# Gate vectors as matmul columns spread by DMA, six shared score sets in the first chunk, an output tail in halves, and a new order

## The chip, the cores and the metric

One core of a Trainium2 chip. The metric is the device time of one execution in microseconds (us), lower is better. The kernel before takes 344.02 us (median of 3 runs, 342.9 to 345.37). TensorE does the matmuls, ScalarE the exponentials and tanh, VectorE and GpSimd the elementwise work. SyncE issues all transfers (DMA), in order, from one queue.

## The reference

```python
mod = (silu(c) @ w_mod).reshape(1, 6, 1, -1)          # c: 1 x 640, w_mod: 640 x 3840
sa, ca, ga, sb, cb, gb = six vectors of 640           # shift, scale, gate, twice
h = layernorm(x) * (1 + ca) + sa                      # x: 2048 x 640, bf16
x = x + ga * (window_attention(h) @ wo)               # 32 heads of 20, each row sees the last 256
h = layernorm(x) * (1 + cb) + sb
x = x + gb * ((sigmoid(h @ w_gate) * (h @ w_up)) @ w_down)   # 640 -> 1536 -> 640
```

The two gate vectors `ga` and `gb` multiply columns of the output, so the kernel multiplies them once into the weights `wo` and `w_down`. For that it keeps each gate copied to all 128 partitions of SBUF (`gbc`, 128 x 640).

## The kernel before

The kernel is a list of operations with what each reads and writes. A planner in the program places them, before anything runs, on the five engines with a model of their durations. Among those that are ready it takes the one with the lowest number in a table of priorities, `TIMES`. The result is a fixed order per engine. Each engine's program is in that order, with waits on semaphores of the others, so a late transfer stops an engine at the first instruction that needs it, and all that stands behind it.

A gate was made on all partitions at once: the left operand is silu(c) copied to 128 columns, so the result has 128 equal rows.

```python
def mod_bc(wm, c0, factor, prio):
    for half in range(2):
        ps = Tile(p_M, "modb")                               # one of three accumulator banks
        ... five matmuls: silubc[:, kt, :] (128x128) by wm[:, kt, 320 columns] -> ps (128x320)
        A("dve", tensor_scalar(gbc[:, 320 columns], ps, factor, mult))
```

The shift and scale vectors are made as columns (`mod_cols`): 25 matmuls of 64 columns, each with a 128 x 128 block of `w_mod` as weights, so that value number t*128 + p lands in partition p, column t. Then come the products with the weights, on whichever of two engines the planner finds free:

```python
for t in range(5):
    A(("pool", "dve"), tensor_tensor(wo[:, t, :], wo[:, t, :], gbc, mult), reads=[wo loads, gbc], tag="wos")
```

The scores of an attention chunk go through one score buffer (four banks) in sets. q and k go to DRAM as `dq<-stg`, `dk<-stg` and come back in another layout, from a few staging buffers `stg`. Attention output goes out as `doc<-On` and comes back as `oT<-doc`. Twenty warm-up matmuls (`S<-Tn`), from 1.36 to 9.3 us in the profile, keep TensorE busy while the first loads are on their way.

The softmax here doesn't subtract the row's maximum and nothing guards it: scores larger than these inputs give would overflow.

## Time and profile before

| | before |
|---|---|
| median time | 344.02 us (3 runs) |
| span of the profiled execution | 339.9 us, mean granted clock (share of TensorE's full speed) 0.999 |
| TensorE busy | 330.0 us, 97% |
| first projection matmul | 13.20 us |
| waits of TensorE | 3.8 us before 14 us, 2.8 us after |
| landing of 128 KB `dq<-stg`, 160 KB `x` | 3.2 us, 4.1 us |

A landing is the time from the issue of a transfer to its completion, as the median over its kind. Two lines of the page's part on DMA issues: the columns are what goes where, the issuing engine, how many, the size of each, and the median landing in us. In all lines of the profile PE is TensorE, DVE VectorE, ACT ScalarE, POOL GpSimd, and SPq the queue of SyncE; L and a number is a line of the kernel.

```profile
x<-in_A_x_dram SPq DMA_DIRECT2D x32, 160.0 KB, 4.1
...
dq<-stg SPq DMA_DIRECT2D x15, 128.0 KB, 3.2
```

The reader is to keep 3 to 5 us in mind as what such transfers take in this kernel: in the busy stretch from 60 to 90 us the medians are 5.0 us for `dq<-stg` and 3.4 for `x`.

### The profile page before, as it was taken

What the parts mean: (1) busy time and instruction counts of PE and PEld (TensorE: products, weight loads), DVE (VectorE), ACT (ScalarE), POOL (GpSimd) and SP (SyncE); (2) the same over time, 40 slices, a digit from 0 to 9 for tenths busy, and PEclk for the clock granted to TensorE, in tenths of its full rate; (3) what the DMA queues carried; (4) which work ended last, traced back from release to release, by engine and by line L of the source; (5) the groups of instructions that cost most, each with busy time, mean ns of one, the idle gap of its engine ahead of it and who ended that gap; (6) DMA issues with size and microseconds to landing.
All of it is one profiled execution on the core that took longest, in us unless ns stands there. A gap on an engine that the chain in (4) does not pass through costs nothing.

```text
span 339.9 us, 9584 instructions
## 1 busy us (share of the span) xinstructions
PE 330.0 (97%) x3813; PEld 201.2 (59%) x3813; DVE 227.6 (67%) x493; ACT 226.9 (67%) x229; POOL 178.4 (52%) x301
## 2 busy tenths in 40 slices
PE   7799989999999999998999999999999999999996
PEld 2577646655555656564765433466545446788884
DVE  4576599999776889646977446398746874554432
ACT  1377878888888888896887798956678851022230
POOL 5132564797666999555675566656656850010000
PEclk9999999999999999999999999999999999999999
DMA  6966689889987752472064101302740122112101
GB/s 211 353 202 181 191 235 257 288 270 209 231 282 253 224 194 41 151 226 60 2 180 115 48 31 65 111 3 40 162 123 12 49 22 72 44 35 41 39 3 39
DMA packets 50990, 44.99 MB, mean 132 GB/s; under 512 B 16513, under 2 KB 46850, under 8 KB 50946
## 3 DMA queue, kind: packets, MB, share of 16 engines
q1 hardware_dynamic: 50946, 44.38, 45.4%
q8 instruction: 30, 0.49, 0.6%
q14 instruction: 14, 0.11, 0.1%
HBM read 28.90 MB, written 12.19 MB: 121 GB/s over the span
## 4 chain that ended last, share of the span: by engine, by line
PE 92%; DMA 4%; SPq 1%; DVE 1%; ACT 1%; issue 0%; ACTq 0%; DVEq 0%
PE M L842 74%; PE S L843 8%; PE O L843 7%; PE M L843 3%; DMA big<-in_w_mod_dram 2%; DMA oT<-doc 1%; SPq L764 1%; DMA doc<-On 1%; ACT hT L984 0%; DVE x L937 0%; DVE V L1020 0%; DVE hT L1005 0%; ACT stg L1019 0%; DVE x L1316 0%; DVE big L1306 0%
## 5 line engine op out<-in xcount | busy, mean ns | idle before, releaser
L1188 ACT ACTIVATE E<-S 128x2048 bf16<-128x2048 f32 (+1 forms) x64 | 118.0, 1844 | 20.9 <-PE S L843 19.6
L842 PE MATMUL M<-h2T,wgu 128*128 128x256 bf16 (+1 forms) x720 | 114.6, 309 | 0.0
L842 PEld LDWEIGHTS M<-h2T,wgu 128*128 128x128 bf16 x720 | 67.2, 98 | 36.6 <-issue 5.5
L1199 POOL TENSOR_SCALAR_AFFINE_SELECT E<-E 128x512 bf16<-128x512 bf16 x89 | 59.9, 683 | 23.3 <-ACT E L1188 21.6
L1201 POOL TENSOR_SCALAR_AFFINE_SELECT E<-E 128x512 bf16<-128x512 bf16 x78 | 50.4, 655 | 31.8 <-ACT E L1188 27.5
L1306 DVE SCALAR_TENSOR_TENSOR big<-sig,M 128x256 bf16<-128x256 f32 (+1 forms) x72 | 36.4, 506 | 41.7 <-PE M L842 20.2
L1304 ACT ACTIVATE sig<-M 128x256 f32<-128x256 f32 (+1 forms) x72 | 32.4, 452 | 44.1 <-PE M L842 43.5
L842 PE MATMUL M<-wd,big 128*128 128x320 bf16 x384 | 56.5, 299 | 0.0
L842 PEld LDWEIGHTS M<-wd,big 128*128 128x128 bf16 x384 | 36.5, 98 | 16.0 <-issue 1.7
L843 PE MATMUL S<-QT,KT 20*128 20x256 bf16 (+2 forms) x832 | 36.2, 258 | 0.0
L926 DVE BATCH_NORM_STATS2 st<-x 128x6 f32<-128x320 bf16 x64 | 27.3, 477 | 7.2 <-DMA x<-in_A_x_dram 7.1
L1249 DVE STREAM_TRANSPOSE T<-O 128x512 f32<-128x512 f32 x32 | 22.6, 708 | 12.6 <-PE O L843 12.5
L843 PEld LDWEIGHTS S<-QT,KT 20*128 20x128 bf16 x832 | 12.3, 92 | 26.5 <-ACT E L1188 9.4
L1316 DVE TENSOR_TENSOR x<-M,x 128x320 bf16<-128x320 f32 x32 | 15.5, 484 | 18.3 <-PE M L842 17.8
L842 PE MATMUL M<-wv,hT 128*128 128x320 bf16 x160 | 27.4, 300 | 0.0
L842 PE MATMUL M<-wo,oT 128*128 128x320 bf16 x160 | 25.8, 300 | 1.5 <-DMA oT<-doc 1.4
L932 POOL TENSOR_SCALAR st<-st 128x2 f32<-128x2 f32 (+1 forms) x11 | 3.0, 274 | 40.4 <-DVE st L929 40.4
L842 PE MATMUL M<-hT,wk 128*128 128x512 bf16 (+1 forms) x100 | 23.1, 354 | 1.1 <-DVE V L1020 1.0
L1258 DVE STREAM_TRANSPOSE On<-Tn 128x512 bf16<-128x512 bf16 x32 | 22.5, 704 | 0.5
L842 PE MATMUL M<-hT,wq 128*128 128x512 bf16 (+1 forms) x100 | 22.7, 356 | 0.0
L843 PE MATMUL O<-E,V 128*32 128x256 bf16 (+2 forms) x568 | 21.1, 262 | 0.0
L1019 ACT ACTIVATE stg<-M 128x512 bf16<-128x512 f32 (+1 forms) x31 | 16.5, 534 | 6.6 <-PE M L842 6.2
(85 smaller groups left out, 386.3 us busy)
## 6 DMA issues: line engine op xcount, KB each, us to landing
x<-in_A_x_dram SPq DMA_DIRECT2D x32, 160.0 KB, 4.1
big<-in_w_mod_dram SPq DMA_DIRECT2D x15, 320.0 KB, 5.5
doc<-On SPq DMA_DIRECT2D x16, 256.0 KB, 2.2
KT<-dk SPq DMA_DIRECT2D x6, 512.0 KB, 5.1
QT<-dq SPq DMA_DIRECT2D x6, 512.0 KB, 4.7
out_dram<-x SPq DMA_DIRECT2D x16, 160.0 KB, 1.8
wgu<-in_B_w_gate_dram SPq DMA_DIRECT2D x5, 384.0 KB, 4.1
dq<-stg SPq DMA_DIRECT2D x15, 128.0 KB, 3.2
```

Of the source, the lines that this page charges most:

```text
L842: return e.matmul(o, l, r, start=st, stop=sp, skip_group_check=True)
L843: return e.matmul(o, l, r, start=st, stop=sp, tile_position=tp, skip_group_check=True)
L926: ins = e.bn_stats(v(bi * 12 + j * 6, 6), src[bi].ap[:, j * 320:(j + 1) * 320])
L1019: return e.activation(dst(), src(), ACT.Copy)
L1188: A("act", lambda e, eng, E=E, Sp=Sp, ncol=ncol: e.activation(E.ap[:, :, 0:ncol], Sp.ap[:, :, 0:ncol], ACT.Exp, scale=SM_SCALE), c_act(4 * ...
L1199: return e.affine_select(ap, ap, pattern=[[0, 4], [1, 128]], compare_op=ALU.is_ge, fill=0.0, base=0, channel_multiplier=-1)
L1201: return e.affine_select(ap, ap, pattern=[[0, 4], [-1, 128]], compare_op=ALU.is_ge, fill=0.0, base=-1, channel_multiplier=1)
L1249: A("dve", lambda e, g: e.transpose(T1.ap[:], O.ap[:]), 0.71, reads=[O.r()], writes=[T1.r()], prio=4, tag="tr1")
L1258: A("dve", lambda e, g: e.transpose(On.ap[:, half * 512:half * 512 + 512], Tn.ap[:]), 0.71, reads=[Tn.r()], writes=[On.r(half)], prio=7, t ...
L1304: A("act", lambda e, g, pg=pg, sg=sg: e.activation(sg.ap[:, 0:W], pg.ap[:, 0:W], ACT.Tanh, scale=0.5), c_act(W), reads=[pg.r()], writes=[s ...
L1306: A("dve", lambda e, g, pu=pu, sg=sg, ft=ft: e.scalar_tensor_tensor(out=hv(ft), in0=sg.ap[:, 0:W], scalar=1.0, in1=pu.ap[:, 0:W], op0=ALU. ...
L1316: A("dve", lambda e, g, ps=ps, bi=bi, half=half: e.tensor_tensor(x1[bi].ap[:, half * 320:half * 320 + 320], ps.ap[:, 0:320], x1[bi].ap[:, ...
```

## The change

The intent: fewer TensorE columns for the gates, two exponentials fewer, a shorter landing at the end, and an order planned anew for all that, with lower rates for some transfers in the planner's model. The diff, cut to its core (the 300 lines of new priorities are left out):

```diff
+HBM = {"qkr": 240.0, "oT": 260.0, "transp": 230.0, "pad": 190.0, "qkw": 275.0}
-                hbm = max(acc + 0.8, hbm) + o.nbytes / 300e3
+                hbm = max(acc + 0.8, hbm) + o.nbytes / 1e3 / HBM.get(o.tag, 300.0)
 TIMES = {   ... all values new ...
     def mod_bc(wm, c0, factor, prio):
-        for half in range(2):
-            ... five matmuls of 320 columns with silubc as weights, tensor_scalar to gbc ...
+        gd = dram(f"gate{c0}", [D])
+        ps = Tile(p_M, "modg")
+        col = mod_cols(wm, c0, ps, prio)
+        A("dve", tensor_scalar(gcol[:], col(), factor, None, op0=ALU.mult), ...)          # 128 x 5
+        dma(gd.rearrange("(t p) -> p t", p=128), gcol[:], 1280, nd=640, nonc=True, tag="gw")
+        dma(gbc[:], bass.AP(gd.tensor, gd.offset, [[0, 128], [1, D]]), 163840, tag="gr")
@@ attention, chunk 0
-                sets = [x for g in gs for x in pieces_of(i0, QB, [g])]      # eight sets of 384 columns
+            for g in range(0, NG, 4):                                       # six sets of 512
+                sets += [[(g, 0, 0, 2), (g, 1, 1, 1), (g + 1, 1, 1, 1)],
+                         [(g + 1, 0, 0, 2), (g + 2, 0, 0, 2)],
+                         [(g + 3, 0, 0, 2), (g + 2, 1, 1, 1), (g + 3, 1, 1, 1)]]
@@ output of the last block
-            dma(out block <- x1, 163840)
+            two writes of 81920, each after its half of the last addition
```

## The prediction

From the trace of the kernel before: 40 matmuls of 64 columns took 1.18 us (10.40 to 11.58), 29.5 ns each, on which the 0.03 us of the start rests; those of 320 columns start 136 to 137 ns apart (and last 299 each, so they overlap); the shortest landings are 1.8 us (`out`) and 2.2 (`doc`).

> **What bounds the kernel now.** I read the page first (busy shares, the chain that ended last, the groups), then TensorE's own waits, then TensorE's instructions in order of time.
>
> ```profile
> PE 330.0 (97%) x3813; PEld 201.2 (59%) x3813; DVE 227.6 (67%) x493; ACT 226.9 (67%) x229; POOL 178.4 (52%) x301
> ...
> PE 92%; DMA 4%; SPq 1%; DVE 1%; ACT 1%; issue 0%; ACTq 0%; DVEq 0%
> ```
>
> The span is 339.9 us (the profiled execution took 341.9, the median is 344.0). TensorE is busy 97% and holds 92% of the chain; the others have a third or more free. Busy alone proves little for pipelined matmuls, so I asked what TensorE waited for:
>
> ```profile
> PE M L842 <- DMA big<-in_w_mod_dram: 2.0, 2, 1.0
> PE M L842 <- DMA oT<-doc: 1.4, 1, 1.4
> PE M L842 <- DVE V L1020: 1.4, 2, 1.0
> PE S L831 <- POOL Tn L786: 1.4, 1, 1.4
> PE M L842 <- ACT hT L984: 0.4, 1, 0.4
> ```
>
> That is all. The first, fourth and fifth fall in the first 13 us, before the projections start. After that only about 2.8 us are real waits: 0.36 us at 18.0 and 1.03 at 48.9 (an accumulator bank that VectorE had not emptied) and 1.41 at 156.0 (the attention output coming back from DRAM). So the rest should be pure instruction stream, and its unit costs can be read off:
>
> ```profile
> 36.89 2.21 PE L842 MATMUL M<-wv,hT 128*128 128x320 bf16 x15
> 39.03 0.34 PE L843 MATMUL S<-QT,KT 20*128 20x256 bf16 x8
> 39.31 2.35 PE L842 MATMUL M<-hT,wq 128*128 128x512 bf16 x10
> ```
>
> Columns are start, time, engine, line, operation, count. From 36.89 to 39.03 are 2.14 us for 15 x 320 = 4,800 columns; ten of 512 columns at the pace 0.43 ns per column would take 2.20, and 4,800 take 2.06, which leaves 0.08 us for the change into the four-row-tile mode of the scores. The score set runs from 39.03 to 39.31 = 0.28 us for (4 x 256 + 4 x 128)/4 = 384 columns, four tiles side by side: 0.165 us at the same pace and 0.115 for the change back. A fit over all the stream gives 0.43 ns per column and 0.09 to 0.12 us per change of tiling mode, whichever two modes.
>
> The ledger then: by the instruction order, with tiled matmuls counted as a quarter, 704,005 columns, of which 14,725 lie before the first projection; 689,280 x 0.43 ns = 296.4 us. 237 changes of mode x 0.10 = 23.7. Start 13.2 (first projection), end 2.8 (last matmul to end of span). Sum 336.1; the missing 3.8 us of the span are the 2.8 of waits and about 0.6 of short ones, and 0.4 of rounding. The kernel is bound by columns and mode changes in TensorE's order; other engines count only where they make TensorE wait.
>
> [...]
>
> **The change part by part.**
>
> Gate vectors. Each of the two gates was two chains of five 320-column matmuls, replicated over 128 rows, with two VectorE evictions each; now 25 matmuls of 64 columns, one small eviction, and two DMAs (640 elements of 2 bytes to DRAM, then broadcast to 128 rows).
>
> ```profile
> L842 PE MATMUL M<-silubc,big 128*128 128x64 bf16 x100 | 3.9, 193 | 2.0 <-DMA big<-in_w_mod_dram 2.0
> L842 PE MATMUL M<-big,silubc 128*128 128x320 bf16 x20 | 3.2, 299 | 0.0
> L904 DVE TENSOR_SCALAR gbc<-M 128x320 bf16<-128x320 f32 x4 | 2.0, 492 | 0.8 <-PE M L842 0.7
> ```
>
> TensorE: minus 20 x 320 = 6,400 columns, plus 50 x 64 = 3,200: net minus 3,200 x 0.43 = -1.4 us, all of it on the path. VectorE: four times 0.49 out, two of some 0.16 in (as the other small evictions of mod columns): -1.6 us, off the path, except that it is short of time between 40 and 80 us (7.2 to 7.9 us busy of each 8). The DMA detour is new latency: write about 3 us (as q and k pieces of 128 KB), read about 4 (as x blocks), so 7 us estimated. The products wo and wd with the gate are far away: by the new order the first gate is done near 60 us and the first output projection stands near 83 (before near 70); wd is needed near 130 and its gate is done near 97. Hidden.
>
> Score sets of the first chunk.
>
> ```profile
> L1188 ACT ACTIVATE E<-S 128x2048 bf16<-128x2048 f32 x59 | 110.8, 1877 | 20.6 <-PE S L843 19.4 <-POOL E L1201 0.7 <-POOL wk L1201 0.2
> ...
> L1188 ACT ACTIVATE E<-S 128x1536 bf16<-128x1536 f32 x5 | 7.2, 1447 | 0.2 <-PE S L843 0.2
> ```
>
> Eight exponentials of 1.45 us become six of 1.88: 11.6 to 11.3 us of ScalarE. Score and value matmuls keep number and shape (352 each of 128 and 256 columns in both). What it takes away is two turns of the single score buffer; in this chunk TensorE had other work in every turn. I give it 0 directly.
>
> New order. All priorities are new, so the whole order moves. Counted: 246 mode changes against 237, +9 x 0.10 = +0.9 us. (Score to value directly 35 against 33, value to full array 48 against 37: the value matmuls are less often glued to others of their mode.)
>
> Start. Now the mod columns of the first matrix all wait for the piece loaded last: 50 matmuls after it instead of 40, +10 x 0.03 = 0.3 us; and only one of the first five transposed blocks is evicted by VectorE, four by ScalarE at 0.56, before two and three. Together +0.5 us.
>
> Tail.
>
> ```profile
> 334.40 1.58 DVE L1316 TENSOR_TENSOR x<-M,x 128x320 bf16<-128x320 f32 x3 [3.33 <-PE M L842]
> 335.51 2.45 SPq L764 DMA_DIRECT2D out_dram<-x  x2
> 337.11 0.49 DVE L1316 TENSOR_TENSOR x<-M,x 128x320 bf16<-128x320 f32 x1 [1.14 <-PE M L842]
> ```
>
> The last addition ends at 337.60 and the span at 339.9: issue and landing of 160 KB, 2.3 us. Half the bytes save only the moving: 80 KB at the 350 GB/s that the second slice of the page shows is 0.23 us. -0.2.
>
> Waits. Of the old ones, 3.4 us in all, the one on oT should go: 10.8 us stood between the last value matmul of that chunk and its output projection on my ledger, now 12.4 (before, 10.8 + 1.4 were needed). New ones: the closest two score sets of 2,048 columns start 2.38 us apart in the trace, which is what exp (1.88) and two handovers need. The new order has eight places closer than that on the ledger: 1.94, 1.98, 2.09, 2.28, 2.28, 2.34, 2.35, 2.35, short by 1.4 us in all. About 0.5 for the second half of the transposed blocks near 18 us (ten matmuls in a row through three banks), 0.3 more for the next five near 28, which overlap the first of the eight, 0.3 for a value bank that must be transposed before the next value matmul, 0.3 for the last oT (10.0 us of cover against 10.5 before, which just sufficed). Sum 2.8 to 2.9 against 3.4: -0.5.
>
> Sum: -1.4 + 0.9 + 0.5 - 0.2 - 0.5 = -0.7 us, 344.0 to 343.3.
>
> **The rivals.** (1) The re-planned order, made with lower DMA rates for some transfers in its planning, removes nearly all waits. On the ledger it can't give more than 1.4 - 0.9 + 3.4 + 0.2 = 4.1 us: 340. For it: the oT wait goes; against it: the close score sets. (2) The gate detour comes late: its 1,280 B are 640 pieces, and later DMAs of the same queue stand behind its wait; should wo be late by 5 us, TensorE has projections to do, but the in-order queue stops at the first wo matmul: 346 to 349. Against it: over 20 us of cover. (3) VectorE or the three accumulator banks stop TensorE more often in 15 to 60 us, where ScalarE and VectorE are both near 80% to 90%: +2 us, 345 to 346. (4) The gain of fewer exponentials is real because ScalarE paces the attention: against it, in the waits of TensorE there is none on exp but weight loads of at most 0.4 us.
>
> **Range and chances.** Columns and mode changes are counted, so their sum (-0.5) is sure within 0.3. The waits can fall anywhere from 0.5 to 6 us, so from -3 to +3; the three runs before spread over 2.5 us. Range 340.5 to 346.2. Two per cent is 6.9 us: for faster, no such amount of waits exists; for slower, a late gate would be needed. Faster 0.02, same 0.95, slower 0.03.
>
> **What would show it.** The 320-column group with silubc gone and 150 matmuls of 64 columns; TensorE's busy time about 0.5 us less than before; first projection at 13.5 to 14; no wait on oT at the third chunk; short waits before scores (score buffer) in 26 to 107 us; last landing some 2.1 us after the last addition. Wrong if TensorE waits for gbc or wo at all, if the waits after 14 us exceed 6 us or fall under 1, or if its pace per column or mode change differs.

## The result, and the profile after

| | before | after |
|---|---|---|
| median of the six runs each on the same chip | 343.79 us (342.9 to 345.37) | 375.23 us (371.13 to 376.49) |
| ratio, 95% interval | | 1.088, 1.082 to 1.094 |
| span of the profiled execution | 339.9 us | 371.1 us |
| mean granted clock | 0.999 | 0.963 |

A ratio here and below is the mean time of one kernel's fast runs over the mean of the other's of the same rounds, so it is not quite the ratio of the medians that are quoted. Executions over 1.5% slower than the fastest of the same kernel are left out of the means. The prediction was wrong: 9% slower, where it gave "slower" 3 chances in 100.

The page of the changed kernel, in the same places as the page of the kernel before: busy times, the granted clock in 40 slices (in tenths), and who holds the chain that ended last.

```profile
PE 334.2 (90%) x3815; PEld 202.9 (55%) x3843; DVE 230.1 (62%) x492; ACT 227.2 (61%) x227; POOL 176.5 (48%) x300
...
PEclk9999999986899858999999999999999999999999
...
PE 73%; DMA 14%; issue 3%; DVE 3%; ACT 2%; POOL 2%; SPq 2%; POOLq 0%; DVEq 0%; ACTq 0%
```

The work of the engines is almost what it was. TensorE's share of the chain has fallen from 92% to 73%, and transfers hold 14%. What TensorE waited for says which (engine, line and tile, what it waited for: us in total, times, longest):

```profile
PE M L849 <- DMA x<-in_A_x_dram: 10.6, 1, 10.6
PE M L849 <- DMA dq<-stg: 9.6, 1, 9.6
...
PE M L850 <- issue: 2.1, 1, 2.1
...
PE M L849 <- DVE V L1028: 2.1, 2, 1.9
```

Neither of the two long waits is for the gate. One is for a block of x, the other for a staging buffer whose content was on its way to DRAM. TensorE's instructions around the second (start, length, what):

```profile
76.67 0.45 PE L849 MATMUL M<-wv,hT 128*128 128x320 bf16 x2
86.76 1.02 PE L849 MATMUL M<-hT,wk 128*128 128x512 bf16 x2 [9.64 <-DMA dq<-stg]
```

The transfers between 66 and 87 us show why. First the GB/s in 40 slices of that stretch, then the landings:

```profile
GB/s 300 339 234 204 200 326 330 348 365 278 280 197 49 25 23 25 69 13 23 9 21 4 15 19 0 0 5 14 25 23 28 44 55 22 0 0 0 0 0 0
...
x<-in_A_x_dram SPq DMA_DIRECT2D x2, 160.0 KB, 16.5
...
dq<-stg SPq DMA_DIRECT2D x2, 128.0 KB, 17.8
gbc<-gate SPq DMA_DIRECT2D x1, 160.0 KB, 4.2
```

The rate drops from some 300 GB/s to under 70 near 72 us and stays low for 12 us; in part that is because the queue issued nothing from 71.1 to 86.4 us. But transfers issued before that, which took 3 to 5 us, now take 16 to 18. The chain of waits names what was under way in that time (start, length):

```profile
67.49 18.94 DMA gate<-gcol
86.45 4.24 DMA gbc<-gate
...
119.28 15.96 DMA x<-in_A_x_dram
```

The first gate's 1,280 bytes were issued at 67.5 us, and the read that waits for them could go out only 18.9 us later. In the trace of the packets all 640 pieces were taken up between 70.8 and 73.2 us, about 9 ns each. Their completion came 13 us later, and packets of other transfers lengthened meanwhile: eight 1 KB packets, where the median is 46 ns, took 2.9 to 10.5 us. The second gate, issued at 118.9, landed after 16.2 us and did the same to the load of x. The waits of VectorE and of the issuing queue, in that order:

```profile
DVE wo L1375 <- DMA gbc<-gate: 14.3, 1, 14.3
```

```profile
SPq L771 <- DMA gate<-gcol: 30.1, 2, 15.4
```

VectorE stood 14.3 us at the product of `wo` with the gate, and the queue 30 us at the two reads. After three of its stops TensorE ran at half clock for a while. Two 20 us windows: busy time of each engine (instructions), then granted clock, DMA share and GB/s:

```profile
80.00:100.00 20.00, 10.95 (x108) 5.19 (x111) 7.77 (x12) 6.16 (x7) 8.24 (x11) 0.66 0.65 148
...
120.00:140.00 20.00, 9.19 (x72) 4.30 (x72) 5.88 (x13) 6.71 (x6) 5.15 (x9) 0.69 0.92 63
```

By the clock's records it was 0.5 from 79.8 to 90.1, 93.5 to 96.9 and 127.6 to 141.3 us, 27.3 us in all. TensorE stood still in the first 7.0 us and in 7.9 us of the last. So it worked for 12.4 us at half clock, which lost 6.2 us: matmuls of 320 columns in a row started 267 ns apart there, and 136 elsewhere. After the stops at 16.5 and 107.7 us no half clock followed.

The sum: from 13 us on, the stops of TensorE over 1.2 us, from one matmul's start to the next, are 9.94, 10.85, 2.37, 2.16 and 1.37, together 26.7. With 6.2 of half clock that is 32.9. The kernel before had 1.33 and 1.68 of such stops. The difference, 29.9, is nearly the 31.2 us between the spans.

Of the smaller steps, the gates' group and the small evictions, and the last addition:

```profile
L849 PE MATMUL M<-silubc,big 128*128 128x64 bf16 x150 | 6.2, 193 | 1.1 <-DMA big<-in_w_mod_dram 1.1
...
L909 DVE TENSOR_SCALAR gcol<-M 128x5 bf16<-128x5 f32 x2 | 0.3, 153 | 0.0
```

```profile
368.49 0.49 DVE L1332 TENSOR_TENSOR x<-M,x 128x320 bf16<-128x320 f32 x1 [0.54 <-PE M L849]
```

The 320-column chains are gone and 150 matmuls of 64 columns stand there, as predicted. The addition ends at 368.98 and the span at 371.1: 2.1 us, as predicted.

### The profile page after: what moved, and what is told of

Its sections match the earlier page's. It is cut to its first block, busy times and chain, and to the rows that moved or that the text cites. A ratio compares the mean times of both kernels' runs of the same rounds, so it can differ in the third digit from the quotient of the medians.

```text
span 371.1 us, 9610 instructions
## 1 busy us (share of the span) xinstructions
PE 334.2 (90%) x3815; PEld 202.9 (55%) x3843; DVE 230.1 (62%) x492; ACT 227.2 (61%) x227; POOL 176.5 (48%) x300
## 4 chain that ended last, share of the span: by engine, by line
PE 73%; DMA 14%; issue 3%; DVE 3%; ACT 2%; POOL 2%; SPq 2%; POOLq 0%; DVEq 0%; ACTq 0%
PE M L849 58%; PE S L850 6%; DMA x<-in_A_x_dram 5%; DMA gate<-gcol 5%; PE O L850 5%; PE M L850 2%; PE S L838 2%; SPq L771 1%; ACT E L1196 1%; DMA big<-in_w_mod_dram 1%; DMA gbc<-gate 1%; DVE st L934 1%; DMA dk<-stg 1%; DMA KT<-dk 1%; DVE x L945 1%
## 5 line engine op out<-in xcount | busy, mean ns | idle before, releaser
L1196 ACT ACTIVATE E<-S 128x2048 bf16<-128x2048 f32 x64 | 120.1, 1877 | 38.2 <-PE S L850 34.3
L849 PE MATMUL M<-h2T,wgu 128*128 128x256 bf16 (+1 forms) x706 | 112.5, 308 | 1.6 <-issue 0.8
L1209 POOL TENSOR_SCALAR_AFFINE_SELECT E<-E 128x512 bf16<-128x512 bf16 x91 | 59.6, 666 | 45.4 <-ACT E L1196 43.6
L1211 POOL TENSOR_SCALAR_AFFINE_SELECT E<-E 128x512 bf16<-128x512 bf16 x80 | 53.3, 678 | 23.5 <-ACT E L1196 23.2
L849 PE MATMUL M<-wo,oT 128*128 128x320 bf16 x160 | 28.1, 318 | 10.6 <-DMA x<-in_A_x_dram 10.6
L850 PE MATMUL S<-QT,KT 20*128 20x128 bf16 (+2 forms) x832 | 36.2, 260 | 0.7 <-ACT E L1196 0.3
L849 PE MATMUL M<-wv,hT 128*128 128x320 bf16 x160 | 28.4, 310 | 2.1 <-DVE V L1028 1.9
L1293 DVE TENSOR_TENSOR x<-M,x 128x320 bf16<-128x320 f32 x32 | 15.2, 484 | 21.5 <-PE M L849 21.5
L1332 DVE TENSOR_TENSOR x<-M,x 128x320 bf16<-128x320 f32 x32 | 15.5, 485 | 19.0 <-PE M L849 18.7
L849 PEld LDWEIGHTS M<-wo,oT 128*128 128x128 bf16 x160 | 15.6, 103 | 19.8 <-issue 12.1
L940 POOL TENSOR_SCALAR st<-st 128x2 f32<-128x2 f32 (+1 forms) x11 | 2.8, 250 | 43.6 <-DVE st L937 40.1
L849 PE MATMUL M<-hT,wq 128*128 128x512 bf16 (+1 forms) x91 | 21.1, 364 | 1.5 <-issue 0.9
```

The costliest lines, as they stand in the source:

```text
L849: return e.matmul(o, l, r, start=st, stop=sp, skip_group_check=True)
L850: return e.matmul(o, l, r, start=st, stop=sp, tile_position=tp, skip_group_check=True)
L1196: A("act", lambda e, eng, E=E, Sp=Sp, ncol=ncol: e.activation(E.ap[:, :, 0:ncol], Sp.ap[:, :, 0:ncol], ACT.Exp, scale=SM_SCALE), c_act(4 * ...
L1209: return e.affine_select(ap, ap, pattern=[[0, 4], [1, 128]], compare_op=ALU.is_ge, fill=0.0, base=0, channel_multiplier=-1)
L1211: return e.affine_select(ap, ap, pattern=[[0, 4], [-1, 128]], compare_op=ALU.is_ge, fill=0.0, base=-1, channel_multiplier=1)
L1293: A("dve", lambda e, g, ps=ps, bi=bi, half=half: e.tensor_tensor(x1[bi].ap[:, half * 320:half * 320 + 320], ps.ap[:, 0:320], x1[bi].ap[:, ...
```

## The experiments

Theory A, formed from this reading: the write of 640 pieces of 2 B lands late and holds up other transfers. Its rivals: B, only the in-order queue's wait for it costs; C, the new order and the other parts of the change cost. Fifteen runs in four batches. The kernel before had a median of 343.44 us in the first batch, 343.26, 345.33 and 345.18 in the others (the last two on another chip), so ratios are what is compared between batches.

### Batch 1: is it the write?

**e1_old_gate**: the changed kernel with the old gate.

```diff
-        col = mod_cols(wm, c0, ps, prio) ... two DMAs
+        for half in range(2): ... five matmuls of 320 columns, tensor_scalar to gbc
```

> The changed kernel with the gate vectors made as before (replicated matmuls, no DMA), all other parts and priorities of the change kept. Theory A (the two 640-piece writes are slow, some 16 us each to land, and hold what is queued behind them) expects 341 to 346 us. Theory B (the order-keeping queue stops at the wait of the gate's read) also expects 341 to 346. Theory C (the new order and the six shared score sets are at fault, the gate comes on top) expects over 355.

Measured 353.24 us, ratio 1.0285 (1.0244 to 1.0326), clock 0.985 in the profile. Most of the loss is gone, but 10 us stay. Theory A's number (341 to 346) is missed.

**e2_gate_rows**: the changed kernel, but the gate's column is turned by one more matmul with the identity, so that it is written as 5 pieces of 256 B. The read, the waits and the order stay.

```diff
+        mm(pt[0:5, 0:128], gcol[:], ident[:]);  tensor_copy(grow, pt)
-        dma(gd.rearrange("(t p) -> p t", p=128), gcol[:], 1280, nd=640, nonc=True)
+        dma(gd.rearrange("(t p) -> t p", p=128), grow[:], 1280, nd=5, k=5)
```

> The changed kernel, but the 128x5 gate column is turned by one small matmul into 5 rows of 128 and written to DRAM as 5 pieces of 256 B instead of 640 of 2 B; the broadcast read and all its waits stay. A expects 341 to 346 and the write to land in 2 to 3 us. B expects over 350, since the queue still waits for the write. C expects over 355.

Measured 351.16 us, ratio 1.023 (1.0178 to 1.0282). The same bytes by the same path in fewer pieces take back 24 of the 31 us. A's number is missed again, and B's "over 350" is met, so this run alone doesn't refute B. By the completion marks the two writes landed after 6.0 and 3.3 us, later than A's 2 to 3, and VectorE still waited 3.4 us for `gbc`.

**e3_write_nobody_reads**: the kernel before plus two such writes of another 128 x 5 tile to spare DRAM, planned for 65 and 98 us. Nothing reads them and nothing waits for them.

```diff
+    dma(spare.rearrange("(t p) -> p t", p=128), siluc[:], 1280, nd=640, nonc=True, tmin=65.0)   # and 98.0
```

> The kernel before, with two additional 640-piece writes of a constant column to spare DRAM at about 65 and 98 us; nothing reads them, no instruction waits for their data. A expects 352 to 370: transfers queued behind the write are held though nobody waits for it, landings of 15 to 18 us behind each. B and C expect 343 to 346 (two more DMA issues).

Measured 387.01 us, ratio 1.1251 (1.1171 to 1.1331), more than A's 352 to 370. The landing of the two writes, and TensorE's waits:

```profile
probe<-siluc SPq DMA_DIRECT2D x2, 1.2 KB, 18.6
```

```profile
PE M L842 <- DMA dq<-stg: 12.7, 1, 12.7
PE M L842 <- DMA x<-in_A_x_dram: 7.6, 1, 7.6
PE M L842 <- DMA oT<-doc: 6.7, 2, 5.6
```

The first two are the kinds of waits seen after the change, here in the old order and with the old gate. That refutes B: no reader stood in the queue for these two writes, 2,560 bytes in all, and they cost 43.6 us.

**e4_gate_part_alone**: the kernel before with the new `mod_bc` alone.

> The kernel before, with only the gate part of the change (columns, 640-piece write, broadcast read); order otherwise planned with the old priorities. A and B expect 360 to 380, the whole loss. C expects 343 to 350.

The two fast runs took 389.13 and 391.45 us, ratio 1.1366 (1.1288 to 1.1444), more than the 360 to 380 of A and B; the median of all four runs, two of them slow, is 393.62. The profiled run took 657.47 us, so its trace isn't used. The gate part by itself costs more than the whole change. The order of the whole change was planned with the detour in it; that this is the reason isn't shown.

What follows: A holds for about 24 of the 31 us. Some 8 to 10 us are not the write.

### Batch 2: what is the rest, and what makes the write slow?

**f1_row_gate_old_order**: e4 with the row write of e2.

> The kernel before with the gate part alone, its column turned by one small matmul into five rows of 128 and written as 5 pieces of 256 B; all other priorities are the old ones. Theory R (what is left of the loss without the slow write, 7.7 us in the run that kept the new order with row writes, belongs to the new order): 342 to 346, the same as before, no wait over 1 us on gbc or stg buffers. Rival G (the detour through DRAM itself costs, the later gbc holding VectorE): 347 to 352, with VectorE waiting several us for gbc and TensorE then for accumulator banks.

Measured 352.21 us, ratio 1.0269 (1.02 to 1.0338). Theory R falls. The detour costs 9 us in the old order too, with many middle-sized waits: TensorE waited 2.5 us for x, 2.0 for oT, 1.5 for `dq<-stg`, 1.2 for the products with `wo`. The time is rival G's, but not its mechanism: VectorE waited only 0.4 us for `gbc`, where G had several.

**f2_six_sets_old_order**: the kernel before with the six shared sets alone (the loop over sets as in the diff above).

> The kernel before with the six shared score sets of the first chunk alone; priorities of all other instructions are the old ones. Theory R: 342.5 to 346, same, no gain, because ScalarE's exponentials were not what TensorE waited for. Rival S (sharing a set between two O banks makes the value matmuls wait or the stream break): 346 to 350, with waits of TensorE between 20 and 60 us that the kernel before does not have.

Measured 347.33 us, ratio 1.0094 (1.003 to 1.0159) over the three fast runs (345.92 to 347.33). It is no gain, and about 3 us of loss, as rival S has it, though within the 2% that count as the same. The profiled run was slow, so I don't say which wait takes them, and the waits that S expects aren't shown.

**f3_new_order_alone**: the kernel before with the new `TIMES` and the new rates.

```diff
-    "score0@a0": "1587 1795 2920 3179 3392 3665 3841 3869",
+    "score0@a0": "2764 3031 3050 3281 3565 3828 3850 4165",     # eight sets need two values more, so do exp0 and mask0
 ... all other priorities as in the changed kernel; old gate, eight sets
```

> The kernel before with the new priorities and the new planning rates alone: old gate, eight score sets (the two sets that had none take values in between), whole last block. Theory R: 350 to 354, as the run with the old gate in the new order (353.2), with the stop of about 2 us near 17 to 19 us and the half clock after it. Rival (the parts cost, not the order): 342 to 346.

Measured 357.4 us, ratio 1.0403 (1.0353 to 1.0452), above both expectations. The order planned for the changed kernel is bad for the instructions of the old one: TensorE stops four times between 98.9 and 107.4 us, on exponentials and on `w_mod`, and has half clock for 13.7 us after the first of these stops. So parts and order are no terms of a sum here; each was fitted to the other. That is why the next batch repairs single waits and keeps the order.

**f5_three_writes_in_the_quiet**: three small writes in the kernel before's last stretch, where there is little traffic (3 to 72 GB/s by the page's slices).

```diff
+    probe("pbyte", dst "(t p) -> p t", tmin=283)                     # 640 pieces of 2 B, side by side
+    probe("pfar",  dst [[256, 128], [256*128, 5], [1, 1]], tmin=303)  # 640 pieces of 2 B, 512 B apart
+    probe("prow",  dst "(p t) -> p t", tmin=318)                     # 128 pieces of 10 B, side by side
```

> The kernel before plus three writes that nobody reads in its quiet last stretch: near 283 us 640 pieces of 2 B side by side (pbyte), near 303 us 640 pieces of 2 B each 512 B apart (pfar), near 318 us the same 1,280 B as 128 pieces of 10 B (prow). If the number of short pieces makes it slow: pbyte 14 to 17 us to landing, pfar the same, prow 4 to 5. If pieces that share the same 512 B hinder each other: pbyte 14 to 17, pfar 2 to 5, prow between. If it was only the traffic near 70 us that made the gate's write slow: all three 2 to 4. The time 344 to 360, no claim hangs on it.

357.25 us. The landings, and last the reads `oT<-doc` of the kernel before in the same stretch:

```profile
pbyte<-siluc SPq DMA_DIRECT2D x1, 1.2 KB, 18.0
oT<-doc SPq DMA_DIRECT2D x4, 80.0 KB, 14.4
```

```profile
oT<-doc SPq DMA_DIRECT2D x4, 80.0 KB, 2.0
```

pbyte landed after 18.0 us, and the reads behind it took 14.4 instead of 2.0, which stopped TensorE for 11.4 us. pfar, with as many pieces of the same size, was complete by 2.2 us after its issue by the trace's completion marks, and a write of the output that was issued 0.4 us before it landed in 1.9. prow was complete within 2.6. So it is neither the number of pieces nor the traffic alone. It is that the pieces of 2 B are close together.

### Batch 3: two repairs, and closer to the cause

**g1_split_warmup** needs a word ahead. The stop of 2.1 us that the waits call "issue" (nothing that the profile shows) stands here in the changed kernel:

```profile
16.21 0.61 PE L850 MATMUL M<-hT,wq 128*32 128x256 bf16 x16
18.92 0.29 PE L850 MATMUL M<-hT,wq 128*32 128x256 bf16 x4 [2.10 <-issue]
```

Counting matmuls from the start, it stands right after the 221st, and in e1, e2 and f3 at exactly the same count, though the times and matmuls differ. Each time a packet of 16 KB of the queue called "instruction" (30 in the kernel before, 0.49 MB) had just begun (16.18 us here, 16.11 in e2, 16.59 in f3), and TensorE went on 1.2 to 1.5 us after that packet had ended. In the kernel before, score sets and transposes stand between, and the 221st matmul comes at 19.5 us, 1.5 us after the packet's end. g1 is e2 with the warm-up cut finer, so that the count runs ahead of the work:

```diff
-        for k in range(1): matmul(S[:, 0, :], Tn[:, 0:128], Tn[:, 0:512])
+        for k in range(6): matmul(S[:, 0, lo:hi], Tn[:, 0:128], Tn[:, lo:hi])    # lo, hi: sixths of 512
```

> The run with row writes (351.2), each of the 20 warm-up matmuls of 512 columns before the load of weights is done cut in six, so that the same columns are 100 more instructions; all else in the same order. In every run that stops near 17 to 19 us (changed kernel, old gate, row writes, six sets, order alone) the stop stands right after the 221st matmul of the stream, whichever matmul that is, and begins some 0.6 us after a 16 KB packet of the instruction queue. Theory I [...]: the place moves with the count, to the 121st of the old numbering near 14 us, where the stream is slower, so a stop of at most 1 us there, none near 17 to 19 us, no half clock at 20 to 24 us, and the time 347 to 349.5. Rival (that matmul waits for something that the profile doesn't show): a stop of 1.9 to 2.2 us before the same matmul as before, time 350 to 352.

Measured 348.89 us, ratio 1.0118 (1.0068 to 1.0167) against e2's 1.023. No stop over 1.2 us is left between 12 and 50 us, and gone is the half clock at 20 to 24 us. The 221st matmul now comes at 14.5 us, 2.8 us after the packet's end, and nothing stops there. A hundred matmuls more made the kernel about 1.1% faster (the two runs are on different chips, and their intervals just don't overlap). That is what theory I expects: the place of the stop goes with the count of instructions. The rival, a wait that belongs to one matmul, is refuted. What TensorE waits for at that count is not in the trace.

**g2_three_more_writes**: as f5, the first two with a reader of one element, so that a wait shows the landing.

```diff
+    probe("pline", 640 pieces of 2 B, 64 B apart, tmin=283)
+    probe("pfew",  128 pieces of 2 B, side by side, tmin=300)
+    probe("pfour", 640 pieces of 4 B, side by side, tmin=318)
```

> The kernel before plus three writes in its quiet last stretch, the first two each followed by a read of one element that waits for it, so that the landing is shown: pline, 640 pieces of 2 B each 64 B apart (planned near 283 us); pfew, 128 pieces of 2 B side by side in 256 B (near 300); pfour, 640 pieces of 4 B side by side (near 318). The write of 640 pieces 512 B apart did not hold anything, the one of 640 side by side took 18.0 us. If pieces hinder each other only within a small line of 64 B: pline 2 to 3 us; if within 512 B: pline 5 to 18. If each piece in a shared line costs its turn: pfew about 128/640 of 16 us plus 2, 4 to 6 us; pfour again 14 to 18 us with what is issued after it held up. No claim hangs on the time, 344 to 360.

353.0 us. pline landed after 4.3 us (2 to 3 were expected), of which its issue took 2.0. pfew was the surprise, in the waits of the queue:

```profile
SPq L764 <- DMA pfew<-siluc: 16.7, 1, 16.7
```

A fifth of the pieces take the same time. The expected 4 to 6 us were the estimate, for a time that goes with the pieces of the whole write (128/640 of 16 us, plus 2). It fits better that the time goes with the pieces in 64 B, which are 32 in both writes. pfour was complete about 9 us after its issue by its completion marks, where 14 to 18 were expected.

**g3_ten_byte_pieces**: the changed kernel and its order, with the weight columns taken with a step of five, so that value p*5 + t lands in partition p, column t, and each partition writes 10 B in one piece.

```diff
-   weights: wm[:, kt, c0 + cg*128 : c0 + cg*128 + 128]
+   weights: wm[:, kt, c0:c0+640].rearrange("p (a b) -> p b a", b=5)[:, cg, :]
-   dma(gd.rearrange("(t p) -> p t", p=128), gcol[:])
+   dma(gd.rearrange("(p t) -> p t", t=5), gcol[:])
```

> The changed kernel in its own order, but the weight columns of the gate taken with a step of five, so that each partition's five results are neighbours in DRAM and the write is 128 pieces of 10 B instead of 640 of 2 B; nothing else differs. As the 128 pieces of 10 B held nothing up in the quiet stretch: landing of the gate's write 2 to 5 us, no wait of TensorE on dq<-stg or x of 9 us, 349 to 354, as the run with row writes (351.2). If it is any write of short pieces next to each other under traffic: a landing over 8 us and 360 to 375.

Measured 352.76 us, ratio 1.0216 (1.0186 to 1.0246). No matmul, no eviction and no DMA more, and the repair is as good as e2's. Its two writes landed after 7.9 and 5.2 us, later than the 2 to 5 expected: under traffic these pieces of 10 B took longer than the 2.6 us of the quiet stretch (f5). No wait of TensorE reaches 3 us.

**g4_tail_halves_alone**: the kernel before with the last block's output in halves.

> The kernel before with the last block's output in two halves alone. Prediction's term: 0.2 us less, so a ratio of 0.999 to 1.001 and, in the trace, 2.1 us from the end of the last addition to the end against 2.3. Rival (the two writes side by side land later than one): 2.3 to 2.6 us. A gain of more than 0.3% is expected by neither.

Measured 344.18 against 345.33, ratio 0.997 (0.9935 to 1.0004). In its trace 2.05 us pass from the end of the last addition (340.35) to the end of the span (342.4). But the last addition itself came late:

```profile
339.86 0.49 DVE L1316 TENSOR_TENSOR x<-M,x 128x320 bf16<-128x320 f32 x1 [1.76 <-DMA out_dram<-x]
```

It stood until the write of the first half of the same tile had landed, 0.66 us after the last matmul's end (0.04 in the kernel before). From the last matmul's end to the end of the span it is 3.17 us here, 2.82 in the kernel before and 2.65 in the changed one. So in this execution, in the old order, the halving made the tail longer. The interval holds the predicted 0.9994; a larger gain isn't excluded, and I claim none.

### Batch 4: what was still open

In g1 two stops over 1.5 us are left, each followed by half clock. One is here. The lines are VectorE's first, TensorE's below:

```profile
78.37 0.49 DVE L1383 TENSOR_TENSOR wo<-wo,gbc 128x640 bf16<-128x640 bf16 x1 [2.84 <-DMA gbc<-gate]
```

```profile
82.10 0.45 PE L852 MATMUL M<-wv,hT 128*128 128x320 bf16 x2 [2.46 <-DVE V L1036]
```

VectorE stands at the product with the gate, which the planner thought would be there by then. The eviction behind it comes late, and TensorE waits for its bank. The other ends at 118.8. The profile of g1 names no cause for it; in g3 TensorE waits at the same place 2.2 us for a load of `wgu`, and such loads stand in the queue behind the read of the second gate.

**h1_planner_knows_landing**: g1 with one number of the planner's model changed.

```diff
-                o.end = bw + (0.9 if o.wr else 1.3)
+                o.end = bw + (4.0 if o.tag == "gw" else 0.9 if o.wr else 1.3)
```

> The run with row writes and the warm-up cut in six (348.9, 1.2% over before), with one number changed in the planning model: the gate's write is taken to land 3.1 us later than the model said, near the 4 us or so that its reader was seen to wait. The planner then moves the gbc read and what hangs on it by itself. Theory D (the rest of the loss is VectorE and the queue waiting for the gate to come back): the 2.5 us wait of TensorE for a bank near 82 and the 1.4 us stop near 118 go, with the half clock after each; 343 to 346. Rival (new order as such, other waits take their place): 347 to 350.

Measured 347.16 us, ratio 1.0087 (1.0037 to 1.0137). Both stops are gone and the granted clock is 1.0 in the profile, so the waits went as theory D said. The time fell less: in microseconds it is the rival's 347 to 350. The kernel before ran at 345.2 on this chip and not at 343.4, on which the numbers rested, but as a ratio too D's upper end (346 over 343.4, 1.0076) is just missed. New waits of 1.1 and 1.0 us took a part of the place, on an addition and on a gated product of VectorE. g1's interval (1.0068 to 1.0167) overlaps this one, so a gain in time isn't shown.

**h3_landing_and_scaling_later**: h1 with the five products of `wo` later.

```diff
-    "wos@w": "7762 7431 7639 7559 7685",
+    "wos@w": "8262 8131 8239 8159 8285",
```

> As h1, and the five products wo by gate get a time 5 to 8 us later in the priorities, so that VectorE does its evictions first. Theory D: no VectorE wait for gbc over 0.5 us, 343 to 346 as h1 or 1 us less. Rival: 347 to 350, with new waits of TensorE on wo.

Measured 346.46 us, ratio 1.0062 (1.0018 to 1.0106), span 343.0 in the profile. The largest named waits of TensorE after 14 us (ten short ones of at most 0.2 us have no name):

```profile
PE S L853 <- ACT E L1204: 1.4, 3, 0.7
PE S L853 <- DMA KT<-dk: 0.8, 1, 0.8
PE M L852 <- DMA dk<-stg: 0.8, 1, 0.8
```

No stop over 1.2 us is left in it. VectorE waited 1.0 us for `gbc`, over theory D's 0.5 (0.4 in h1), and TensorE not at all for `wo`. The change, with three repairs, is then 0.6% slower than the kernel before (interval above zero, but within the 2% that counts as the same). Theory D's 343 to 346 is missed by half a microsecond; as a ratio it is met. From g1's 1.2% to 0.6% the direction is D's, though the intervals overlap.

**h4_pieces_per_line**: three writes as in g2, all with a reader.

```diff
+    probe("peight", 640 pieces of 2 B, 8 B apart, tmin=283)
+    probe("pten",   128 pieces of 10 B, side by side, tmin=298)
+    probe("ptwo",   640 pieces of 2 B, 4 B apart, tmin=315)
```

> The kernel before plus three writes in the quiet last stretch, each read back by one element: peight, 640 pieces of 2 B 8 B apart (8 in 64 B), pten, 128 pieces of 10 B side by side (6 to 7 in 64 B), ptwo, 640 pieces of 2 B 4 B apart (16 in 64 B). If the time goes by the number of pieces in one line of 64 B, some 0.45 us each over a floor near 2 us (32 gave 16 to 17): peight 5 to 7, pten 4 to 6, ptwo 8 to 10. If it is only pieces that touch each other: peight and ptwo 2 to 4, pten slow. No claim hangs on the time.

345.08 us. peight landed after 4.8 us by its transfers' landing, a little under the expectation; the other two are waits of the queue, ptwo as expected, pten well under its 4 to 6:

```profile
SPq L764 <- DMA ptwo<-siluc: 8.8, 1, 8.8
...
SPq L764 <- DMA pten<-siluc: 2.5, 1, 2.5
```

All small writes of the three probing runs together. The times run from the issue to the landing, of which the issue is 0.4 to 0.5 us where nothing else is said; those marked * are waits of the queue, which leave the issue out:

| write | pieces in 64 B | us |
|---|---|---|
| 640 x 2 B side by side | 32 | 18.0, of it 2.2 the issue |
| 128 x 2 B side by side | 32 | 16.7* |
| 640 x 4 B side by side | 16 | about 9 |
| 640 x 2 B, 4 B apart | 16 | 8.8* |
| 640 x 2 B, 8 B apart | 8 | 4.8 |
| 128 x 10 B side by side | 6 to 7 | 2.5*, 2.6 in f5 |
| 640 x 2 B, 64 B apart | 1 | 4.3, of it 2.0 the issue |
| 640 x 2 B, 512 B apart | below 1 | 2.2 |

From 8 to 32 pieces of 2 or 4 B in 64 B it is about 0.5 us for each piece more (an estimate from the table: 4.8, 8.8 and 16.7 us for 8, 16 and 32), and it was about the same whether the write covers 4 times 64 B or 20 (16.7 us, and 15.8 without the issue). That 64 B is the right length to count in isn't shown: pieces 64 B apart hinder one another little, if at all (without the issue 2.3 us, against 1.7 at 512 B). The count alone doesn't give the time either, as pieces of 10 B are faster than it has them (2.5 us for 6 to 7, against 4.8 for 8 of 2 B). Why pieces close together wait isn't shown: the traces show only the completions.

No kernel is shown to be faster than the kernel before. g4 is the nearest, and it is the same within its interval.

## Why the prediction was wrong, by its own steps

**The step that failed** is the sentence on the gate's detour: "write about 3 us (as q and k pieces of 128 KB), read about 4 (as x blocks), so 7 us estimated", with "Hidden" behind it. Three things in it were off. The write's size was taken from transfers with large pieces; with 32 pieces of 2 B in 64 B it took 16.2 and 18.9 us. No term of the sum comes of the size of the pieces. The cost was thought to be the gate's own lateness, while in fact other transfers were held, which needs no reader at all (e3); in the changed kernel TensorE stood 9.6 us for `dq<-stg` and 10.6 for `x`. And the cover of "over 20 us" was counted to the first matmul with `wo`, while the first to need the gate is the product on VectorE, which came to it 9 us after the write was issued (76.5 and 67.5 us) and has evictions behind it, and the read in the queue, with loads behind it. Even after the write was cured, that second kind of waiting was there: when the planner was told of it (h1, h3), the two stops went, and the ratio went from 1.012 to 1.009 and 1.006, with intervals that overlap.

**Rival (2)** named the late gate and the 640 pieces, and put 346 to 349 on it. It thought of the queue alone and of 5 us. The landing of 16 to 19 us, the held transfers and the half clock (6.2 us) make it 31 us, where this rival has 2 to 5.

**Columns and mode changes** (-0.5) were right as far as can be seen. The groups have the predicted counts, the traces have 237 and 246 changes of mode as counted, and between stops the pace is the same in both: matmuls of 320 columns in a row start 136 ns apart, of 256 columns 109. That its busy time would be 0.5 us lower was not seen: it rose by 4.2 us, since matmuls at half clock take twice as long (and 28 matmul records are missing from that trace, 3,815 against 3,843 weight loads).

**Start** (+0.5): the part that was counted was right, and two others were not seen. From the matmuls on the last piece of `w_mod` to the first projection it took 3.21 us instead of 2.80, 0.4 more. But these matmuls began at 9.56 us instead of 10.40, so the first projection came at 12.77, 0.4 earlier than before, and not at 13.5 to 14; that this is more than chance isn't shown. The loss came after it, the 2.1 us stop after matmul 221. In e2, where half clock follows it (in the changed kernel none did), it cost about 1.1% (e2 against g1).

**Tail** (-0.2): right in the changed kernel, 2.1 us for 2.3. That the second half's addition can be held by the first half's write, as in g4, is not in the prediction.

**Waits**: that the wait on oT at the third chunk would go was right; it isn't in the list. The close score sets, sized 1.4, cost 0.3 (the wait of scores for exponentials). The others were small beside what was not foreseen.

**Exponentials** (0): there was no gain, as said, but f2 shows a loss of 0.3% to 1.6% in the old order, which the ledger did not have.

**The range** came from "the waits can fall anywhere from 0.5 to 6 us". It was made from the waits that the kernel before has. The one new kind of transfer should have widened it upwards.

What stays open: what costs the 9 us of f1, where VectorE hardly waits for the gate, which waits make up f2's loss, and why the new order is so bad for the old instructions (f3) beyond the waits named. Why TensorE stopped after the 221st matmul isn't shown; g1 shows only that the place goes with the count.

## What to carry to other kernels

Never write a column of single 2-byte values so that they come to lie side by side in DRAM: arrange the matmul so that each partition holds neighbours, or turn the column first; five-element pieces took 2.5 us where single ones took 16 to 18 (5.2 and 7.9 where 16.2 and 18.9 under traffic), and the slow write held up transfers that had nothing to do with it (in the changed kernel `dq<-stg` of 128 KB landed after 17.8 us, where the median before was 3.2). When you ask whether a new transfer is hidden, count the cover to the first instruction of each in-order queue that waits for it, not to the first use in the algorithm, and let the planner's model know its measured landing. A stop of TensorE can cost nearly twice its length: after stops of 2.16 us (changed kernel), 2.21 (e1) and 1.61 (g1) came 3.41 us of half clock, which lose another 1.7 us. After stops of 1.68 (kernel before), 2.37 (changed kernel) and 3.40 (e2) none came, so no length that is safe is shown.
